# A linear-attention kernel with a GELU layer on one core: longer clock warm-up, tiled filler products, the first level's copy moved off VectorE, and a new order for the first two loops

## The chip, the core and the metric

The kernel runs on one core of a Trainium2 chip. The core has a matrix engine (TensorE, here PE; its weight loads are listed as PEld), a vector engine (VectorE, DVE), an engine for activations and copies (ScalarE, ACT), GpSimd (POOL) and SyncE (SP), which issues most of the transfers. Each engine works through its own instructions in the order in which the program emits them, and waits at semaphores for the others. The metric is the device time of one execution in microseconds (us), lower is better.

## What is computed

The first half is an attention without softmax: for each batch and head a 48 x 48 state decays by a factor per row and step, and takes in one outer product per step. The second half is a layer of two matrix products with an exact GELU between them.

```python
for t in range(S):                       # batch 4, heads 8, S = 768, D = 48
    kt, vt, rt, wt = (k[:, :, t], v[:, :, t], r[:, :, t], w[:, :, t])
    cur = np.einsum('bhd,bhe->bhde', u[None] * kt, vt)
    y[:, :, t] = np.einsum('bhd,bhde->bhe', rt, state + cur)
    state = wt[:, :, :, None] * state + np.einsum('bhd,bhe->bhde', kt, vt)
x = y.transpose(0, 2, 1, 3).reshape(3072, 384)
h = x @ w_in                             # 384 x 2048
out = (0.5 * h * (1.0 + erf(h / sqrt(2)))) @ w_out   # 2048 x 384
```

## The kernel before

**Tiles.** The 768 steps of each of the 4 batches are cut in two, so there are 8 tiles of 384 steps for all 8 heads (`x` from 0 to 7). `attention(x, unit)` computes the attention of one tile, `mlp(x)` the two products with the GELU behind it. Tile 0 is cut again into two units of four heads each (`units_of`), so that its parts can overlap while there is no other work yet; from tile 1 on a tile is one unit, and its attention runs beside the `mlp` of the tile before it.

**Attention.** Inside a chunk of 64 steps the matrix of scores is built by levels (`halves`, L469, for tiles 0 and 1): level h (1, 2, 4, 8, 16, 32) covers the pairs of steps in the two halves of blocks of 2h. For each level PE multiplies k by r in quadrants of 64 x 64 (`products`, L445), the needed part of the result `d` is copied from PSUM into the score matrix `a_sb`, and DVE multiplies r and k by the decay of their block (`update`, L493 to L505), so that the next level can use them in place. A level's update has to wait for its product, and the next product for the update. For levels 1 to 8 the copy is a predicated copy by DVE with a byte mask (L516); for levels 16 and 32 it is a row of plain copies by ACT (L513). The diagonal, with u, has a product of its own (L461) and a predicated copy (L465), which follows level 1's copy. Before the levels ACT scales r by u (L401) and DVE forms the products of the decays (L411). After them k is transposed (L685, copied by ACT at L687), multiplied with v (L711), the scores are multiplied with v (L752), DVE chains the states over the chunks (L726), and the states are multiplied with r (L797). The results go to `xT`: unit 0's by copies of ACT and DVE (L804), unit 1's by DVE copies (L820) and, for the heads whose rows are spread, through `ysb` (an ACT copy, L823) and six transfers (L827), three issued by SP and three by ACT.

**Fillers.** `keep_warm` (L219) issues products of a tile of zeros, 128 x 128 by 128 x 512, whose result nobody reads. Eight stand in front (L227), two behind each product of a level in tile 0 but the first (L457, twelve times in all), and six at the end of tile 0's loop.

**Weights.** They arrive as 64-bit floats in 16 pieces of 768 columns (8 of w_in, then 8 of w_out), with room for five (`raws`). A piece is brought in by `weight_in`, prepared by three ACT operations (`prepare`, L333 to L336) and finished by two DVE operations (`finish`, a shift at L345 and an add at L349). `conversion` runs these steps and, at its end, issues the piece that comes three later (L318). The first three pieces, and tile 1's r, k and w (`load_second`), are gated: a DVE memset of one column stands before each transfer, so that the transfer starts when DVE has come to that place. In tile 1's loop the products of w_in with a new piece need its add, and ACT's preparations stand in line with the GELUs of the same loop; two PSUM banks take turns under the products of h, so the product of one block waits until the GELU two blocks earlier has read its bank.

**Order.** `PLAN` (L39) holds a string per tile, written out by hand. Each letter runs one step of one stream, up to its next `yield`: for tile 0 "." is unit 0, "s" unit 1, "f" the attention of tile 1, "l" the gated loads, "c" the conversion of weights, "p" the preparation of pieces 1 and 2, "w" the load of tile 1's v, "x" the six fillers at the end. For later tiles "." is the `mlp` of the tile before, "s" the attention of this tile, "f" that of the next, "l" loads, "w" masks and sums, "x" sums of xT. The string fixes the order on every engine and on every queue.

Of the kernel before, what the change touches and what calls it, by code (L numbers as in the profile page):

```python
# [10 lines left out]
F32 = mybir.dt.float32  # L11
# [7 lines left out]
ALU = mybir.AluOpType  # L19
# [13 lines left out]
BANK = 512  # L33
# [3 lines left out]
NC_SP = 8  # L37
HALFWAY = 2
PLAN = {  # L39
    0: "l.s....llsl.lssslslss.lc.l.slslls...ssss..lcs.s.s.l.ss..ss..sccs.c.s.llpssslw..cs.ffpcc",  # L40
    1: (
        "..ccswccc.csl.scscs.s.sccwsc.clccs.ccsccc.csc.lscclswwclc.scs.wcssw.ss.cclcsc.ccs.lclccsc."
        "ccclfccccccfccfcccccfccfccwf.ff......fw.sl.w.x.wx...x..x...xww"
    ),
    2: (
        "s.s.....ss....ssw.ws.wl.wsss.wws.s..lsl...lws.w..s.ww....s.s..l..sss.lssss....s..s..s.sls."
        "llsf.sf.fs..fl.xx.x.fxx"
    ),
    3: (
# [24 lines left out]
def kernel(  # L74
# [9 lines left out]
    nc = tc.nc  # L84
# [16 lines left out]
    ps = ctx.enter_context(tc.tile_pool(name="ps", bufs=1, space=PSUM))  # L101
# [22 lines left out]
    half = [slice(0, 64), slice(64, 128)]  # L124
# [8 lines left out]
    bufs = [io.tile([128, 3 * NP * T], F32, name=f"rkw{i}", bufs=1) for i in range(2)]  # L133
# [58 lines left out]
    def weight_in(i, gate=False):  # L192

        if i < len(pieces):
            dst, src = pieces[i]
            raws[i] = cv.tile([128, PIECE], I64, name="raw", bufs=AHEAD) if wide else None
            if wide:
                dst = raws[i].rearrange("p (a c) -> p a c", a=dst.shape[1])
            if not gate:
                nc.sync.dma_start(out=dst, in_=src)  # L200
                return
            for a in range(dst.shape[1]):
                if wide:
                    nc.vector.memset(dst[:, a].bitcast(U32)[:, 0:1], 0)
                nc.sync.dma_start(out=dst[:, a], in_=src[:, a])
                yield
# [5 lines left out]
    zeros = const.tile([128, BANK], BF16, name="zeros")  # L212
    nc.vector.memset(zeros, 0.0)
    two = const.tile([128, 1], F32, name="two")
# [4 lines left out]
    def keep_warm(n, elsewhere=False):  # L219
        if elsewhere:  # L220
            t = pair("warm")[:, 0]
        else:
            t = ps.tile([128, BANK], F32, name="warm", tag="mm", bufs=2)
        for _ in range(n):
            nc.tensor.matmul(t, lhsT=zeros[:, 0:128], rhs=zeros, start=True, stop=True)

    keep_warm(8)  # L227


    masks = {h: const.tile([128, C // 2], U8, name=f"mask{h}") for h in LEVELS if h < 16}  # L230
# [37 lines left out]
    for i, h in enumerate(QUARTERS[:1]):  # L268
        for a in range(3):
            w_q = (3 - a) * C // 4  # L270
            z = q_ints[1 if a == 0 else 2]
# [35 lines left out]
    def conversion():  # L307

        i = converted[0]
        if i >= len(pieces):  # L310
            return
        converted[0] += 1

        prepare(i + HALFWAY if i > 1 else 0)
        yield
        if wide:
            yield from finish(pieces[i][0], raws[i], *halfway[i])
        for _ in weight_in(i + 3):  # L318
            pass

    def convert():
        for _ in conversion():
# [30 lines left out]
    def attention(x, unit):  # L353
# [7 lines left out]
        base = unit * 3 * n_u  # L361
# [3 lines left out]
        at = a_sb[:, :, parts[0] * NI:(parts[0] + np_) * NI]  # L365
# [79 lines left out]
        def products(bs, right, width, rest=False):  # L445
            d = pair("d")
            n = 0
            for b in bs:
                for i in range(NI):
                    for g in range(2):  # L450
                        for p in range(2):
                            nc.tensor.matmul(d[half[p], g, n * width:(n + 1) * width],  # L452
                                             lhsT=kc[half[g], b, i, p], rhs=right(half[g], b, i, p),
                                             start=True, stop=True)
                    n += 1
            if x == 0 and not rest:
                keep_warm(2)  # L457
            return d[:, :, 0:n * width]

        def diagonal():  # L460
# [8 lines left out]
        def halves():  # L469

            for h in LEVELS:
                m = C // 2 // h
                if np_ < NPART:

                    d = products(range(np_), lambda z, b, i, p: rc[z, b, i, p], C, h == 1)
                    d = d.rearrange("p g (n m two j) -> p g n m two j", two=2, j=h, m=m)[:, :, :, :, 1, :]
                else:
                    right = rc.rearrange("p b i c (m two j) -> p b i c m two j", two=2, j=h)[:, :, :, :, :, 1, :]
                    d = products(range(np_), lambda z, b, i, p: right[z, b, i, p], C // 2)
                    d = d.rearrange("p g (n m j) -> p g n m j", j=h, m=m)  # L480
                if h == 1:
                    yield
                    diag = diagonal()
                yield

                r2 = r.rearrange("p (n two j) -> p n two j", two=2, j=h)[:, :, 1, :]
                t2 = tot[h].rearrange("p (n two) -> p n two", two=2)[:, :, 0:1].to_broadcast(r2.shape)
                k2 = k.rearrange("p (n two j) -> p n two j", two=2, j=h)[:, :, 0, :]
                tk = tot[h].rearrange("p (n two) -> p n two", two=2)[:, :, 1:2].to_broadcast(k2.shape)
                rk = bass.AP(tensor=r2.tensor, offset=r2.offset, ap=[r2.ap[0], [n_u - h, 2]] + list(r2.ap[1:]))  # L490
                tt = bass.AP(tensor=t2.tensor, offset=t2.offset, ap=[t2.ap[0], [1, 2]] + list(t2.ap[1:]))

                def update(z, r2=r2, t2=t2, k2=k2, tk=tk):  # L493
                    nc.vector.tensor_mul(*((k2, k2, tk) if z is k else (r2, r2, t2)))

                if x == 0 and m == 1:

                    update(k)
                    last_r.append(lambda: update(r))
                elif x == 0 and h == 1:  # L500
                    update(r)
                    yield
                    update(k)
                else:
                    nc.vector.tensor_mul(rk, rk, tt)  # L505
                yield
                ah = at.rearrange("p g n (m two j) -> p g n m two j", two=2, j=h)[:, :, :, :, 1, :]
                if h >= 16:

                    for p in range(2):  # L510
                        for i in range(m):
                            s = slice(p * 64 + i * 2 * h, p * 64 + i * 2 * h + h)
                            nc.scalar.copy(out=ah[s, :, :, i], in_=d[s, :, :, i])  # L513
                else:
                    mask = masks[h].rearrange("p (m j) -> p m j", j=h).unsqueeze(1).unsqueeze(1)
                    nc.vector.copy_predicated(out=ah, mask=mask.to_broadcast(ah.shape), data=d)  # L516
                if h == 1:
                    copy_diagonal(diag)
                yield
# [186 lines left out]
        for b in range(np_):  # L706
            kv_ps = pair("kv_ps")
            for i in range(NI):
                for p in range(2):
                    for g in range(2):  # L710
                        nc.tensor.matmul(kv_ps[half[g], p, i * D:(i + 1) * D], lhsT=k_t(b, i, p, g),  # L711
                                         rhs=vs(b, i, g)[half[p], 0:D], start=True, stop=True)
# [74 lines left out]
        for i in range(NI):  # L787
            for p in range(2):
                for b in range(np_):
                    q, c3 = divmod(i, N3)  # L790
                    for g in range(2):
                        c = 2 * c3 + (p + g) % 2
                        src, c0 = (st, c - 1) if c else (before, NC - 1)
                        if src is None:
# [4 lines left out]
                                         start=False, stop=True, skip_group_check=True)  # L799
# [518 lines left out]
```

## Time and profile before

| | us |
|---|---|
| median of 3 runs | 588.55 (588.53 to 589.37) |
| the profiled execution | 589.61 |
| its span in the profile | 587.8 |
| PE busy, share of the span | 571.1 (97%) |
| DVE busy | 425.5 (72%) |
| ACT busy | 291.2 (50%) |
| POOL busy | 58.6 (10%) |
| PE's mean granted clock | 0.997 |

The span is the time between the first and the last instruction that the profile shows; 1.8 us of the execution lie outside of it. A row of the profile names a line of the kernel, the engine, the operation, and what it writes and reads. A 32-bit product leaves two records of PE, so the 24 products of one level of a unit are listed as x48. Starts are counted from the beginning of the span.

### The profile page before, as it was taken

Reading aid. Unit: us, or ns where it says so; the run is one execution under the profiler, and the core shown is the slowest. Engines: PE = TensorE matmul, PEld = TensorE weight load, DVE = VectorE, ACT = ScalarE, POOL = GpSimd, SP = SyncE. Lnnn points to the kernel's source line nnn. Section 1 sums busy time; section 2 is a strip of 40 time slices with the busy share of each in tenths; the row PEclk is TensorE's granted clock in tenths of the full one; section 3 lists DMA queues with packets and bytes.
Section 4 is the critical chain, followed back from the end, with each engine's and each line's share of the span. In section 5 each row is a group of like instructions: output and inputs, shape, how many; then the busy total and the mean of one; then the engine's idle time right before and its main releaser. Section 6 shows DMA issues by size and latency. Waiting matters only on the chain. (4 is left out here: it accounts for less than half of the span.)

```text
span 587.8 us, 17656 instructions
## 1 busy us (share of the span) xinstructions
PE 571.1 (97%) x7602; PEld 521.4 (89%) x7616; DVE 425.5 (72%) x825; ACT 291.2 (50%) x668; POOL 58.6 (10%) x63
## 2 busy tenths in 40 slices
PE   5789999999999999999999999999999999999997
PEld 3576666799999999999999999999998999999997
DVE  5988968989758975777959986777759987420332
ACT  2368898446362567235462467245561467335400
POOL 3100000013000130012000130002100111003100
PEclk8999999999999999999999999999999999999999
DMA  6749742253032542354122632344224333114201
GB/s 230 221 135 352 265 168 78 79 142 52 5 89 64 157 58 41 90 142 93 26 55 79 151 70 44 86 139 74 27 41 119 86 42 42 29 45 55 28 13 35
DMA packets 62430, 55.09 MB, mean 94 GB/s; under 512 B 32400, under 2 KB 47504, under 8 KB 62352
## 3 DMA queue, kind: packets, MB, share of 16 engines
q1 hardware_dynamic: 50832, 45.62, 25.5%
q0 software_dynamic: 11424, 8.26, 10.8%
q8 instruction: 60, 0.98, 0.7%
q14 instruction: 18, 0.15, 0.1%
q10 hardware_dynamic: 96, 0.07, 0.1%
HBM read 36.24 MB, written 4.72 MB: 70 GB/s over the span
## 5 line engine op out<-in xcount | busy, mean ns | idle before, releaser
L929 PE MATMUL h_ps<-xT,w_in_sb 128*128 128x192 f32 x560 | 111.5, 330 | 0.6 <-DVE o_sb L1196 0.6
L980 POOL DMA_DIRECT2D g<-o_sb x42 | 50.6, 1229 | 478.2 <-ACT o_sb L965 468.9
L929 PEld LDWEIGHTS h_ps<-xT,w_in_sb 128*128 128x128 f32 x560 | 93.0, 190 | 4.7 <-ACT g L961 1.6
L929 PE MATMUL u_ps<-s,w_in_sb 128*128 128x192 f32 x224 | 41.2, 327 | 0.0
L1073 PE MATMUL o_ps<-w_out_sb,g 128*128 128x192 f32 x224 | 39.8, 326 | 0.0
L929 PEld LDWEIGHTS u_ps<-s,w_in_sb 128*128 128x128 f32 x224 | 37.1, 190 | 0.2
L1073 PEld LDWEIGHTS o_ps<-w_out_sb,g 128*128 128x128 f32 x224 | 37.0, 190 | 0.0
L604 ACT COPY a_sb<-d 32x256 f32<-32x256 f32 (+8 forms) x90 | 32.6, 362 | 4.9 <-PE d L588 3.4
L1059 PE MATMUL h_ps<-xT,w_in_sb 128*128 128x384 f32 x96 | 33.2, 494 | 0.0
L452 PEld LDWEIGHTS d<-rkw 64*64 64x64 f32 x1152 | 19.4, 138 | 14.7 <-issue 10.5
L1073 PE MATMUL o_ps<-w_out_sb,f 128*128 128x192 f32 x176 | 32.0, 331 | 0.0
L1073 PE MATMUL o_ps<-t,g 128*128 128x192 f32 x176 | 31.4, 330 | 0.0
L1073 PE MATMUL o_ps<-t,s 128*128 128x192 f32 x176 | 31.2, 328 | 0.0
L1073 PE MATMUL o_ps<-t,e 128*128 128x192 f32 x176 | 30.6, 326 | 0.5 <-issue 0.5
L621 DVE COPY_PREDICATED a_sb<-quarter,d 128x480 f32<-128x480 uint8 (+5 forms) x54 | 23.2, 439 | 10.5 <-PE d L588 9.3
L726 DVE SCALAR_TENSOR_TENSOR st<-st,tot_sb,kv_ps 128x48 f32<-128x48 f32 x160 | 28.9, 258 | 2.6 <-PE kv_ps L711 2.5
L1073 PE MATMUL o_ps<-w_out_sb,e 128*128 128x192 f32 x176 | 30.7, 328 | 0.0
L982 DVE TENSOR_TENSOR g<-g,o_sb 128x384 f32<-128x384 f32 x14 | 7.6, 549 | 31.2 <-ACT o_sb L965 31.1
L1073 PEld LDWEIGHTS o_ps<-t,e 128*128 128x128 f32 x176 | 28.9, 190 | 0.7 <-issue 0.7
L1073 PEld LDWEIGHTS o_ps<-t,g 128*128 128x128 f32 x176 | 28.6, 190 | 0.5
L1073 PEld LDWEIGHTS o_ps<-w_out_sb,f 128*128 128x128 f32 x176 | 28.5, 190 | 0.6
L1073 PEld LDWEIGHTS o_ps<-t,s 128*128 128x128 f32 x176 | 28.8, 190 | 0.2
(163 smaller groups left out, 1171.3 us busy)
## 6 DMA issues: line engine op xcount, KB each, us to landing
rkw<-in_rkw_dram SPq DMA_DIRECT2D x54, 256.0 KB, 3.6
g<-o_sb POOLq DMA_DIRECT2D x42, 192.0 KB, 3.6
raw<-in_w_out_dram SPq DMA_DIRECT2D x8, 768.0 KB, 6.2
v_in<-in_v_dram SPq DMA_DIRECT2D x8, 584.0 KB, 4.6
raw<-in_w_in_dram SPq DMA_DIRECT2D x5, 768.0 KB, 7.5
out_dram<-o_sb SPq DMA_DIRECT2D x20, 192.0 KB, 2.0
rkw<-kx SPq DMA_DIRECT2D x72, 48.0 KB, 2.0
rkw<-in_rkw_dram SPq DMA_DIRECT2D x6, 384.0 KB, 6.2
```

The source lines that it names most:

```text
L452: nc.tensor.matmul(d[half[p], g, n * width:(n + 1) * width], lhsT=kc[half[g], b, i, p], rhs=right(half[g], b, i, p), start=True, stop=True)
L604: nc.scalar.copy(out=at[z, g, first:behind, (a + 1) * h:], in_=d[z, :, :, to] if g == slice(None) else d[z, :, to])
L621: nc.vector.copy_predicated(out=an[:, :, :, :, (a + 1) * h:], mask=mask.to_broadcast(data.shape), data=data)
L726: nc.vector.scalar_tensor_tensor(out=stq[:, q, c], in0=stq[:, q, c - 1] if c else b4[:, q, NC - 1], scalar=totq[:, q, c:c + 1], in1=kvs[q ...
L929: nc.tensor.matmul(o, lhsT=lhsT, rhs=rhs, start=start, stop=True, skip_group_check=True)
L980: nc.gpsimd.dma_start(out=g, in_=z, accum_op=ALU.add)
L982: nc.vector.tensor_add(g, g, z)
L1059: nc.tensor.matmul(h_ps, lhsT=w_in_sb[:, f // FI, j, f % FI * 128:(f % FI + 1) * 128], rhs=xT[:, j, :], start=(j == 0), stop=(j == NJ - 1))
L1073: nc.tensor.matmul(o, lhsT=lhs(j), rhs=rhs(j), start=start and j == 0, stop=(j == HF - 1), skip_group_check=True)
```

## The change

- `keep_warm(24)` in front instead of `keep_warm(8)`.
- The twelve fillers between the levels of tile 0 are four products of 64 x 64 by 64 x 512 each, one in each quadrant of PE, on two banks (`keep_warm_tiles`), instead of two products over the whole array.
- Level 1 in tile 0: the predicated copy by DVE goes. ACT copies the odd columns of `d` into `a_sb` without a mask, and two affine selects of POOL (64 partitions and 384 columns each, one for each half) set to zero what lies below the diagonal; what they leave above it is overwritten by later levels. The diagonal's copy by DVE follows them.
- The fourth piece of weights (number 3) is issued at the end of the second conversion, together with the fifth, instead of at the end of the first.
- The strings of `PLAN` for tiles 0 and 1 are new; that of tile 2 differs in its first slots.

```diff
@@ PLAN @@
-    0: "l.s....llsl.lssslslss.lc.l.slslls...ssss..lcs.s.s.l.ss..ss..sccs.c.s.llpssslw..cs.ffpcc",
+    0: ".s..l.l.lsll..ssl.lslclslls.cs.s.sl.ls.sc.ssspsl..s.sslsl...s.sc.css.l.ccpws.sss..s.cff",
     1: (
-        "..ccswccc.csl.scscs.s.sccwsc.clccs.ccsccc.csc.lscclswwclc.scs.wcssw.ss.cclcsc.ccs.lclccsc."
-        "ccclfccccccfccfcccccfccfccwf.ff......fw.sl.w.x.wx...x..x...xww"
+        ".wcsccc..c.scwssccc.ccsccsl.cwscscs.lll.ccccccss.scccscc.csc.sscsc.clscl.s.ccsc.cscswc.ccl"
+        "llcccflsccw.c.fc.cwccxxc...fwf.x.cc.cf.cc.f......f..fwxfw.wxww"
     ),
     2: (
-        "s.s.....ss....ssw.ws.wl.wsss.wws.s..lsl...lws.w..s.ww....s.s..l..sss.lssss....s..s..s.sls."
+        ".s......sss...ssw.ws.wl.wsss.wws.s..lsl...lws.w..s.ww....s.s..l..sss.lssss....s..s..s.sls."
...
+    def keep_warm_tiles():
+        ts = [ps.tile([128, BANK], F32, name="warm", tag="mm", bufs=2) for _ in range(2)]
+        for p in range(2):
+            for g in range(2):
+                nc.tensor.matmul(ts[g][half[p]], lhsT=zeros[half[g], 0:64], rhs=zeros[half[g]], start=True, stop=True)
-    keep_warm(8)
+    keep_warm(24)
...
-        for _ in weight_in(i + 3):
-            pass
+        for n in (() if i == 0 else (3, 4) if i == 1 else (i + 3,)):
+            for _ in weight_in(n):
+                pass
...
             if x == 0 and not rest:
-                keep_warm(2)
+                keep_warm_tiles()
...
+                ah = at.rearrange("p g n (m two j) -> p g n m two j", two=2, j=h)[:, :, :, :, 1, :]
+                if h == 1 and x == 0:
+                    nc.scalar.copy(out=ah, in_=d)
+                    for z in half:
+                        a1 = ah[z, :, :, :, 0]
+                        nc.gpsimd.affine_select(out=a1, in_=a1, pattern=[[0, 2], [0, a1.shape[2]], [2, m]], base=1,
+                                                channel_multiplier=-1, compare_op=ALU.is_ge, fill=0.0)
...
-                ah = at.rearrange("p g n (m two j) -> p g n m two j", two=2, j=h)[:, :, :, :, 1, :]
                 if h >= 16:
...
-                else:
+                elif h > 1 or x:
                     mask = masks[h].rearrange("p (m j) -> p m j", j=h).unsqueeze(1).unsqueeze(1)
                     nc.vector.copy_predicated(out=ah, mask=mask.to_broadcast(ah.shape), data=d)
```

Read letter by letter, the new strings move the following. In tile 0, the first gated load of weights moves from the very front behind both units' decay products and unit 0's first two products. Unit 0's diagonal copy stands before unit 1's first update, and unit 0's product of level 2 before unit 1's diagonal product. The preparation of piece 1 stands on ACT before the copies of level 16, and that of piece 2 before `ysb`, where they stood behind the copy of the transposed k and behind tile 1's first steps. In tile 1's loop, the add of piece 1 follows the first block of h, pieces 3 and 4 are issued behind it, and the preparation of piece 3 stands before the GELU of the second block. The products of states with r (L797) come before the first product of the second layer, where they came behind nine of them. The sums of weights and of xT are spread later in the loop.

## The prediction

> **What bounds the kernel now.** I read the busy shares first, then the waits of TensorE (PE), then the timeline of the first 60 us.
>
> ```profile
> PE 571.1 (97%) x7602; PEld 521.4 (89%) x7616; DVE 425.5 (72%) x825; ACT 291.2 (50%) x668; POOL 58.6 (10%) x63
> ...
> PE   5789999999999999999999999999999999999997
> ```
>
> PE is busy everywhere except in the first three slices (14.7 us each). Its waits between 40 and 120 us are one of 0.5 us, and after 112 us 1.8 us in all; from 41.5 us (the first products of tile 1) it is a solid block. So the change can gain only what it brings this block forward, and lose what holes it makes in it. TensorE's waits of the first 50 us:
>
> ```profile
> PE d L452 <- DMA rkw<-in_rkw_dram: 3.5, 1, 3.5
> PE warm L225 <- ACT zeros L217: 2.3, 1, 2.3
> PE d L452 <- issue: 1.8, 2, 1.4
> PE kv_ps L711 <- issue: 1.0, 1, 1.0
> ```
>
> "issue" is a wait that no semaphore explains. TensorE's timeline shows where:
>
> ```profile
> 2.29 3.59 PE L225 MATMUL warm<-zeros 128*128 128x512 bf16 x8 [2.29 <-ACT zeros L217]
> 9.43 1.56 PE L452 MATMUL d<-rkw 64*64 64x64 f32 x48 [3.55 <-DMA rkw<-in_rkw_dram]
> ...
> 18.76 0.91 PE L452 MATMUL d<-rkw 64*64 64x64 f32 x45 [0.22 <-DVE rkw L163]
> 21.09 0.33 PE L452 MATMUL d<-rkw 64*64 64x64 f32 x3 [1.42 <-issue]
> ...
> 28.09 0.93 PE L452 MATMUL d<-rkw 64*64 64x64 f32 x48
> 28.95 0.39 PE L225 MATMUL warm<-zeros 128*128 128x512 bf16 x1
> 29.48 0.93 PE L452 MATMUL d<-rkw 64*64 64x64 f32 x48
> ```
>
> The first product takes 1.56, later ones 0.93. The breaks come at 699, 953 and 1717 PE instructions (matmuls plus weight loads, counted from the timeline): 254 and three times 254.7 apart. The instruction queue moved 60 packets, 0.98 MB, so 16 KB each; over the 15,218 matmuls and loads that is 64 bytes an instruction and 256 a packet. In windows of 0.2 us those packets start at 12.8, 18.6, 22.2, 26.6, 30.0, 35.0, mostly 1.0 us after a boundary; PE resumes 4.8 us after one (16.3 to 21.09), 4.5 (21.09 to 25.55), and a boundary at 29.0 passes 3.45 us after. So in this stage PE uses at most a block per 3.4 to 4.8 us, the longer ones while the data queue is full.
>
> Between 14 and 30 us VectorE (DVE) is the other bound: busy 4.97, 4.53 and 4.42 of each 5 us from 15 to 30.
>
> **The clock in front.** Windows of 1 us (seventh figure: granted clock):
>
> ```profile
> 9.00:10.00 1.00, 0.57 (x21) 0.60 (x25) 0.00 (x0) 0.56 (x2) 0.00 (x0) 0.68 0.99 402
> 10.00:11.00 1.00, 1.00 (x50) 1.00 (x46) 0.00 (x0) 0.74 (x2) 0.00 (x0) 0.50 0.85 339
> 12.00:13.00 1.00, 0.67 (x13) 0.22 (x6) 0.67 (x5) 0.00 (x0) 0.00 (x0) 0.61 0.18 62
> 13.00:14.00 1.00, 0.93 (x49) 0.82 (x49) 0.97 (x2) 0.00 (x0) 0.00 (x0) 1.00 0.05 16
> ```
>
> Half clock from 9.36 to 12.78 us, 3.42 us long, after 3.55 us of idleness. Loads of the eight fillers are 0.427 us apart; warm ones 0.216 (six from 43.09 end where the next product starts, 44.40). If the clock rises at 5.95, one span before 9.36, 24 products end at 2.29 + 3.66 + 15.4 x 0.216 = 9.3, just before the data (9.43). The first two products then cost 0.93 each, not 1.56 and 1.54: unit 0's second ends at 11.3, not 12.3. [...] A start up to 10.4 stays hidden behind ScalarE (ACT), below.
>
> **Level 1 by ACT and POOL.** Removed from DVE: two predicated copies of 1.02. Added: two ACT copies of 384 columns (0.48, the row of ysb), four affine selects of 64 x 384.
>
> ```profile
> masks.py:199 POOL TENSOR_SCALAR_AFFINE_SELECT ident<-ident 128x128 f32<-128x128 f32 x1 | 0.3, 295 | 0.1
> L289 POOL COPY rkw<-ident 32x128 f32<-32x128 f32 x4 | 2.4, 589 | 0.2
> ```
>
> The 16-element iota takes 0.17, so 128 elements cost 0.13 of the 0.295 above it; 384 give 0.17 + 0.39 = 0.56. From the strided copy (0.589 per 128) 1.6; from the plain memset (1.38 per 1536) 0.4. I take 0.58, the same operation; two in a row 1.16, bounds 0.8 to 3.2. Unit 0's ACT copy stands behind unit 1's scaling by u, which waits for its r and ends at 11.38 (10.26 + 1.12): 11.38 + 0.48 + 1.16 + 0.2 for two hand-overs = **13.2**. DVE has finished unit 0's updates at 11.9, and its diagonal copy waits there; behind it in order are unit 1's r update and, through that, everything. So 1.3 us of the 2.1 saved return as a wait; with 3.2 all of it and more. Unit 1's selects end at about 14.4, its diagonal copy is due at 16: hidden.
>
> From 13.2, by start-to-start times of the rows (diagonal 0.94, r and k 0.48 each, level 2 updates 0.9, copies 0.9): eight operations, 6.45, end at 19.65 against 21.40 before. Then, for DVE alone, the level 4 and 8 updates and copies (2.8 a level) and the first shift (0.5) end at 25.75, and the last two levels alternate with PE: 29.3 for unit 0's last k update (31.88 before).
>
> **Fillers in tiles.** Twelve times two full products become four 64 x 64 ones. Lower bound 0.22 (side by side), upper 0.86 (in a row). The 48 records of d take 0.93, though 64 columns at the h rate (0.345 per 384) in a row would take 2.76: quadrants do run beside each other. I take 0.25. A step of PE shrinks from 1.395 (28.09 to 29.48) to 1.17, but only where PE sets the pace (26 to 32 us: five steps, 1.1). At upper cost five steps lose 2.
>
> **Instruction blocks.** The change adds 32 instructions in front and 4 per filler, 80 by the end of the levels. Counted back from 699, boundaries lie at 187, 443 and so on. With 48 instructions of fillers and 96 of the first product ahead, 187 is passed at 10.8, inside unit 0's second product (43 of 96), and its block is there at 14.8; 443, reached at 13.5 (after unit 1's first product and unit 0's level 2), waits for it; then 19.1, 23.1, 26.6, 30.1, taking 4.0, 4.3, 4.0, 3.5 and 3.5 from the cycles above, as the loads now fill 11 to 20 us. The boundary at 30.1 lies in the last product of the levels, so its k update starts at 30.3, before 31.88: **1.6 earlier**. DVE alone would reach it at 29.3. [...]
>
> **Loads moved, weights, ACT's queue.** The first weight gate goes behind both totals (DVE 3.2 to 7.7 us; SP 4.57 to about 7.7). The loads land in issue order (k of unit 0 at 9.4, r of unit 1 at 10.2, v 12.6, weights 13.5), so I count 0, at most 0.4. All 17 gates remain, 0.06 each. The second conversion is prepared before the level 16 copies (weights there by 22, ACT done by 25, copies due at 26: hidden). The third preparation (2.95 on ACT) now stands before ysb. Its last third is gated behind the first add: 30.8 + 0.95 = 31.75, landing 3.0 to 3.8 later (35.3), prepared at 38.2. The cross products end at 37.1; so ysb starts at 38.2, before 39.57; behind it on ACT are three xT loads (2.18) and unit 0's xT copies. xT lands 1.4 earlier; PE's own path (chains, cross products, tile 1, six fillers) gives h at 42.4 to 42.8 against 44.40. I take 42.8: **1.6**.
>
> **Tile 1's loop.** Weight piece 3, issued at 30.48 before, now follows the xT loads on SP, at 40.2, and pieces 4 to 7 with it. Its preparation stands on ACT before the gelu of h1, which frees the bank of h3. First of a string, a piece lands after 6.1 or 6.6: 46.6; prepared 49.5, gelu 49.9; h3 is due at 42.8 + 3 x 2.05 + 1.55 = 50.5. Hidden by 0.6. Later, shift 4 waits on DVE for the piece prepared behind h3's gelu; eleven DVE operations follow (11.6) before the level 16 products, due 14.9 after h3; 0.43 + 2.88 + 12.05 = 15.4. I count 0.05 of the possible 0.5, since overlaps of 0.1 per operation undo it. Weights of the second layer: last add about 0.7 us ahead of need, counted 0. Tile 2's order changes only in its first slots: 0.
>
> Sum: -1.6 + 0.05 = -1.55. The profiled execution took 589.61 (span 587.8, 1.8 around it), the median of runs 588.55; a change in the span applies to both. 588.55 - 1.55 = **587.0**.
>
> **Rivals and chances.** Forecast, 0.50: -0.8 to -2.4 (586.15 to 587.75).
> Fetch hides, 0.20: the k update at 29.3, add done 30.75, weights 34.3, ysb 37.2; h at 42.1, 586.2, down to 585.0 if POOL also is quick (1.3 less wait). For it: no break at 29.0 and 34.2. Against: three breaks.
> The gain is spent, 0.17: POOL at 3.2 us (ready at 15.2) delays DVE by 2.0, partly behind PE's block wait; or the hole of 0.5 and small ones. 587.8 to 589.7.
> Slower, 0.13: piece 3 lands late, sharing the queue with pieces 4 to 7 and v. Rows of later pieces are 8.5 and 9.9 us. Decisive from 6.9 after issue (47.1); each us beyond is a us of hole before h3; break-even at 8.5, at 9.9 it costs 3.0 and gives 590.0.
> That the fillers do not warm the clock is part of these: 24 products span 5.2 us even warm.
>
> A measurement here can tell 0.2%, 1.2 us. Faster: 0.7 of the forecast plus the second, 0.55; slower 0.13 and a little of the third, 0.14; same 0.31. The range leaves out the far end of the second (0.05) and most of the fourth: 585.4 to 588.9.
>
> **What would show it.** Right: first product near 9.4 and 0.93 long; a DVE wait of about 1.3 on POOL before the first diagonal copy; breaks of PE 256 instructions apart; ysb right behind the third preparation; h from about 42.8, no PE wait after. Wrong: selects over 1 us each, fillers past 10.4, or a PE wait on the gelu before h3.

## The result: slower by 0.85%

| | before | after |
|---|---|---|
| median of five runs each, us | 588.85 (588.53 to 589.37) | 594.51 (592.88 to 594.53) |
| the profiled execution | 589.61 | 592.88 |
| its span | 587.8 | 591.2 |

The ratio is 1.0085 [1.0072, 1.0098]. The forecast was 587.0 and the range ended at 588.9: wrong, and on the other side. The profiled executions lie only 3.3 us apart, because the traced run of before is longer than any of its five and that of after is its shortest. What follows explains the 3.4 us between the two spans; the further 2 us of the medians rest on runs without a trace, and come up again under the clock.

The busy shares of the changed kernel, as shown for before:

```profile
PE 572.6 (97%) x7654; PEld 522.3 (88%) x7656; DVE 423.8 (72%) x823; ACT 292.1 (49%) x670; POOL 61.0 (10%) x67
...
PE   7679999999999999999999999999999999999997
```

DVE has lost 1.7 us of work, as meant. PE is fuller in the first slice (7 tenths instead of 5) and emptier in the next two (6 and 7 instead of 7 and 8); over the whole span its share is 97% in both. What is lost shows in TensorE's waits (what, released by what: total, times, longest):

```profile
PE d L460 <- issue: 6.5, 5, 1.8
PE warm L225 <- ACT zeros L217: 2.4, 1, 2.4
PE y_ps L813 <- issue: 1.3, 1, 1.3
PE d L460 <- DVE rkw L522: 0.8, 1, 0.8
PE kv_ps L727 <- issue: 0.8, 1, 0.8
PE warm L232 <- issue: 0.7, 1, 0.7
PE h_ps L1075 <- issue: 0.6, 1, 0.6
```

The wait of 3.5 us for the first data is gone, since the 24 products now fill it. In its place stand waits for "issue", which no semaphore explains: nine breaks and 9.8 us in the first 80 us, where before had five and 3.2 (two of these, 0.5 us together, stand ahead of fillers and belong to no boundary). TensorE's timeline shows where they lie (start, busy, what it is, how many, and the idle time ahead of it):

```profile
2.37 8.06 PE L225 MATMUL warm<-zeros 128*128 128x512 bf16 x24 [2.37 <-ACT zeros L217]
10.35 0.93 PE L460 MATMUL d<-rkw 64*64 64x64 f32 x48
...
14.95 0.40 PE L232 MATMUL warm<-zeros 64*64 64x512 bf16 x2 [0.67 <-issue]
...
20.05 0.62 PE L460 MATMUL d<-rkw 64*64 64x64 f32 x25 [1.78 <-issue]
...
24.05 0.27 PE L460 MATMUL d<-rkw 64*64 64x64 f32 x1 [1.35 <-issue]
...
31.39 0.28 PE L460 MATMUL d<-rkw 64*64 64x64 f32 x4 [0.94 <-issue]
...
36.13 0.80 PE L727 MATMUL kv_ps<-v_in,kx 64*64 64x48 f32 x41 [0.76 <-issue]
...
40.13 1.33 PE L813 MATMUL y_ps<-rkw,st 64*64 64x64 f32 x39 [1.33 <-issue]
...
43.87 0.36 PE L460 MATMUL d<-rkw 64*64 64x32 f32 x9 [1.10 <-issue]
...
52.15 3.71 PE L1075 MATMUL h_ps<-xT,w_in_sb 128*128 128x384 f32 x11 [0.57 <-issue]
...
72.96 0.89 PE L460 MATMUL d<-rkw 64*64 64x32 f32 x44 [1.31 <-issue]
```

Each break falls inside a row of equal products, never between two steps, so missing data does not explain it: the next record of the same row is held back. Counted over products and weight loads in the trace, the breaks stand at 445, 701, 957, 1467, 1719, 1975, 2231, 2478 and 3240. So they follow each other at 256 instructions, or at about a multiple of it where a boundary passes without a break (at about 28, 61.5 and 67.5 us); a few records are missing from a trace. The instruction queue again moved 60 packets of 16 KB, and each of the nine breaks ends 2.3 to 2.7 us after one of these packets has started (at 17.66, 21.44 and 28.96 for the breaks that end at 20.05, 24.05 and 31.39).

How far each stage is behind or ahead (starts in us):

| | before | after | difference |
|---|---|---|---|
| first product | 9.43 | 10.35 | +0.9 |
| unit 0's diagonal copy | 13.89 | 13.47 | -0.4 |
| first level 4 update | 21.46 | 20.76 | -0.7 |
| unit 0's last k update | 31.88 | 31.80 | -0.1 |
| `ysb` | 39.57 | 40.38 | +0.8 |
| first block of h | 44.40 | 45.47 | +1.1 |
| fifth block of h | 55.52 | 57.31 | +1.8 |
| tile 2's first product (u) | 118.36 | 122.10 | +3.7 |
| the last row of the second layer | 554.92 | 558.28 | +3.4 |

The saving of the levels is eaten by four breaks inside them (15 to 32 us). Then three breaks between the levels and h, 3.2 us long, cost a net 1.1, since before had a break of 0.96 and a wait of 0.52 in the same stretch. The loop of tile 1 costs another 2.7: from the first h to tile 2's u it takes 76.63 instead of 73.96. Its two breaks are 1.88 of idle time and cost 2.0 with the restart; this is the difference to after_full_apart (below), which has full fillers, the same string but for one step, and no break there. That run still takes 74.62, so 0.66 belongs to the new string itself, half of it in one row of products of the scores with v (1.97 long instead of 1.63). After 122 us nothing is lost any more.

### The profile page after: what moved, and what is told of

The parts are those of the page before. It is cut to its first block, busy times and chain, and to the rows that moved or that the text cites. A ratio compares the mean times of both kernels' runs of the same rounds, so it can differ in the third digit from the quotient of the medians.

```text
span 591.2 us, 17753 instructions
## 1 busy us (share of the span) xinstructions
PE 572.6 (97%) x7654; PEld 522.3 (88%) x7656; DVE 423.8 (72%) x823; ACT 292.1 (49%) x670; POOL 61.0 (10%) x67
## 5 line engine op out<-in xcount | busy, mean ns | idle before, releaser
L460 PE MATMUL d<-rkw 64*64 64x64 f32 (+1 forms) x1152 | 22.3, 221 | 8.1 <-issue 6.5
```

Of the source, the lines that this page charges most:

```text
L460: nc.tensor.matmul(d[half[p], g, n * width:(n + 1) * width], lhsT=kc[half[g], b, i, p], rhs=right(half[g], b, i, p), start=True, stop=True)
```

## Experiments

**Theory A:** PE gets its instructions at no more than a block of 256 per 3.5 to 4 us; the change shifts the boundaries, and adds instructions, so that they fall into dense rows on the path. **Rivals:** B, the tiled fillers themselves take too long; C, they fail to hold the clock; D, the new order of tile 0 or tile 1 loses, whatever the fillers; E, the blocks come late because the data transfers crowd them out. Medians below are of several runs, and each ratio is against before on the same chip. Single runs of one kernel differ by 1.5 to 7.4 us, so only intervals decide. The "issue" column and the starts are of one traced run each.

### Which part of the change costs

The changed kernel once more, and parts of it undone:

> The changed kernel itself, beside the others on one chip: 593 to 594.5 (ratio 1.006 to 1.009); PE breaks of the kind issue of 8 to 11 us in all.

> After, with the old strings of tiles 1 and 2. Theory (blocks of 256 PE instructions that arrive no faster than one per 3.4 to 5.5 us, which the change asks for faster): the hole of 1.31 at 73 us comes from two level products (384 records and loads) only 2.0 us apart, the one of 0.57 at 52 from the late fourth piece; with the old string the level products are 5.6 us apart again, the first hole goes, and the second may stay because the piece is still issued behind xT: 1.3 to 1.9 less than after. Rival (everything is lost before 45 us): same as after within 0.3.

> After, with the old string of tile 0 (its loads and steps in the old order), all else new. Theory of blocks: the fillers and their 80 instructions stay, so PE still breaks every 256 instructions; the data loads of 11 to 20 us come later again, so the breaks get shorter: 0 to 1.5 less than after. Rival (the new order of tile 0 is what costs): h starts about 1 earlier than in after and 1.5 to 3 of the loss goes.

> After, with the twelve fillers between the levels as two full products again. Theory of blocks: 48 instructions fewer before the end of the levels, breaks of PE shorter by about 0.7 in all and others moved: 0.5 to 1.5 less than after. Rival (tiled fillers do not keep the clock up, which is what the runs with a mean clock of 0.988 to 0.997 and spans of 592.8 show): clock 0.997 or more in all runs and 1.5 to 3 less. Second rival (tiled fillers help): 0.5 to 1.5 more, since PE steps of 1.17 become 1.4.

> After, with 8 products in front. In after the 24 end at 10.43 and hold back data that is there by about 9. Theory (the front is a loss of its own): first product 0.9 to 1.4 earlier, but at half clock (1.56 and 1.54 instead of 0.93), 32 instructions fewer: net 0 to 1.5 less than after. Rival (warm clock is worth it): 0.5 to 1.5 more than after.

> After, with the full fillers and the old strings of tiles 1 and 2: what is left of the change is 24 products in front, level 1 by ScalarE and GpSimd, the late fourth piece and the new string of tile 0. Theory of blocks: both places where blocks ran short are gone; -1 to +0.5 against before, breaks under 4 us in all. Rival (new order of tile 0 costs by itself): +1.5 to +3 against before.

```diff
 after_old_loop1:       PLAN[1] and PLAN[2] of before
 after_old_loop0:       PLAN[0] of before
 after_full_fillers:
-                keep_warm_tiles()
+                keep_warm(2)
 after_8_in_front:
-    keep_warm(24)
+    keep_warm(8)
 after_full_old_loop1:  full fillers, and PLAN[1], PLAN[2] of before
```

| | median | ratio [95%] | "issue" to 80 us | first h | tile 2's u |
|---|---|---|---|---|---|
| after_again | 594.14 | 1.0081 [1.0051, 1.0111] | 9.2 | 46.75 | 124.85 |
| after_old_loop1 | 590.72 | 1.0033 [1.0011, 1.0054] | 7.6 | 45.00 | 119.60 |
| after_old_loop0 | 596.28 | 1.0114 [1.0076, 1.0153] | 11.5 | 47.49 | 127.42 |
| after_full_fillers | 590.20 | 1.0022 [0.9997, 1.0046] | 3.9 | 45.20 | 124.78 |
| after_8_in_front | 590.77 | 1.0022 [1.0003, 1.0041] | 5.6 | 44.74 | 120.40 |
| after_full_old_loop1 | 588.93 | 0.9997 [0.9970, 1.0025] | 3.0 | 43.70 | 117.76 |

(The traced run of after_full_fillers was by far its longest, 594.99; its stations count little.)

The loss repeats. Three different edits each take back about 3 us of it (2.8 to 3.5 by the ratios, more than I had expected of any of them): other fillers, the old loop of tile 1, or 16 products (32 instructions) fewer in front. Two of them together take back about 5, all of it, less than the sum of the two. That speaks against a cost that sits in one part, and for one resource that all of them draw on or shift. The new string of tile 0, suspected by rival D, is not shown to lose: with the old one the kernel is no faster (1.0114, four runs, an interval that overlaps that of after_again), where I had expected up to 1.5 us less. Everything else in the change (24 in front, level 1 by ACT and POOL, the later fourth piece, tile 0's order) is together worth nothing that can be measured, 0.9997.

### Instructions, or time of the fillers

> After, with one 64 x 64 product per filler instead of four (2 instructions instead of 8; the same 0.2 us, as the four run side by side). Theory of blocks: 72 instructions fewer before the end of the levels, each stretch between breaks holds more work, 1.5 to 3 less than after. Rival (time of fillers or clock matters): the array is used a quarter as much, so the clock falls more often (mean 0.99 or less) and the time is the same as after or 1 to 3 more.

> Before, with two narrow products of zeros (two columns, 128 x 128) added behind each of the twelve fillers: 8 instructions per filler, as many as the tiled ones, and about 0.1 us of PE. Theory of blocks: breaks grow by about 48 instructions' share of a block (0.7 us) and move: 0.5 to 2 more than before. Rival (instructions do not matter): no more than the 0.1 per step where PE sets the pace, 0 to 0.5 more.

> After, with fillers of two full products and two narrow ones (two columns): 8 instructions like the four tiles, but 0.5 us on the array instead of 0.2. If the tiles lose by their instructions: as after (593 to 594.5), breaks of 8 us or more. If they lose by their short time (a block of 256 instructions is used up before the next is there, PE idles, the clock falls): near after_full_fillers (590 to 591.5), breaks under 5, clock mostly 1.0.

> After with full fillers, and 24 narrow products (64 x 64, two columns, 48 instructions, some 0.5 us in a stretch in which PE waits for ScalarE's copy of the transposed k) in front of unit 1's kv. The levels run as in after_full_fillers, but behind them the boundaries lie where after has them. If the place decides: breaks again with 41, 39 and 9 records left in kv, in the products of the states and in tile 1's first product, and with 44 in tile 1's level 16, 3 to 5 us in all; 1.5 to 3.5 more than after_full_fillers, 591.7 to 593.7. If their number in the levels decides: within 0.7 of after_full_fillers.

```diff
 after_one_tile (one 64 x 64 product per filler, 2 instructions instead of 8):
-        for p in range(2):
-            for g in range(2):
+        for p in range(1):
+            for g in range(1):
 before_more_instructions (before), after_full_padded (after, two full products): 8 instructions per filler
+            nc.tensor.matmul(t[:, 0:2], lhsT=zeros[:, 0:128], rhs=zeros[:, 0:2], ...)   # twice
 after_full_shifted (full fillers; after the transposes of unit 0's k in tile 0, 48 instructions):
+                for _ in range(24):
+                    nc.tensor.matmul(t[half[0], 0:2], lhsT=zeros[half[0], 0:64], rhs=zeros[half[0], 0:2], ...)
```

| | median | ratio [95%] | "issue" to 80 us | first h | tile 2's u |
|---|---|---|---|---|---|
| after_one_tile | 591.79 | 1.0029 [0.9995, 1.0062] | 4.5 | 43.26 | 118.81 |
| before_more_instructions | 590.18 | 1.0005 [0.9979, 1.0032] | 2.4 | 44.62 | 118.58 |
| after_full_padded | 595.18 | 1.0097 [1.0059, 1.0134] | 6.4 | 45.58 | 123.54 |
| after_full_shifted | 594.29 | 1.0084 [1.0053, 1.0115] | 6.1 | 45.42 | 122.73 |

after_one_tile, with fewer instructions, takes back 2.4 us by the medians, as expected; the intervals still touch. after_full_padded has the full fillers, which alone were at 1.0022, and the instruction count of the tiled ones. It is as slow as the changed kernel, though its breaks come to 6.4 us, less than the 8 that I had expected, and it breaks at the same records behind the levels (41, 39, 9 and 44 left, compare the timeline above):

```profile
36.80 0.80 PE L733 MATMUL kv_ps<-v_in,kx 64*64 64x48 f32 x41 [0.77 <-issue]
...
40.25 1.33 PE L819 MATMUL y_ps<-rkw,st 64*64 64x64 f32 x39 [0.79 <-issue]
...
43.99 0.36 PE L465 MATMUL d<-rkw 64*64 64x32 f32 x9 [1.10 <-issue]
...
72.72 0.89 PE L465 MATMUL d<-rkw 64*64 64x32 f32 x44 [1.43 <-issue]
```

after_full_shifted leaves the fillers of the levels alone and puts the 48 missing instructions at a place where PE waits for ACT's copy of k anyway. That wait is only 0.23 us, so they hold kv back by about 0.4. The breaks come back, one record further on, and with them the whole loss (the expectation had 591.7 to 593.7):

```profile
36.59 0.84 PE L731 MATMUL kv_ps<-v_in,kx 64*64 64x48 f32 x42 [0.94 <-issue]
...
40.31 1.33 PE L817 MATMUL y_ps<-rkw,st 64*64 64x64 f32 x40 [1.06 <-issue]
...
43.77 0.41 PE L460 MATMUL d<-rkw 64*64 64x32 f32 x10 [0.72 <-issue]
...
73.59 0.89 PE L460 MATMUL d<-rkw 64*64 64x32 f32 x45 [1.46 <-issue]
```

So rival B falls: the time of the tiled fillers costs nothing that these runs show, their instructions do. And it is not their number as such: before takes the same number per filler without a measurable loss (I had expected 0.5 to 2 more; the interval runs from -1.2 to +1.9). There, 32 instructions fewer stand ahead (8 products in front), and the boundaries lie elsewhere. What decides is which row a boundary falls into.

The sum of the breaks does not decide: after_full_shifted, with 6.1, is as slow as the changed kernel with 9.8, and after_old_loop1, with 7.6, is faster than both. Among the runs built from the changed kernel, the breaks behind the levels come nearer. They are 4.1 to 5.1 us in after, after_again, after_old_loop0, after_full_padded and after_full_shifted (ratios 1.0081 to 1.0114), 2.0 to 2.9 in after_old_loop1, after_one_tile and one_full_old_loop1 (1.0029 to 1.0043), and 1.0 or less in after_full_fillers, after_full_apart, after_full_old_loop1 and full_old_loop1_18 (0.9997 to 1.0022). after_light_loads, with 4.5 at 1.0048, and after_8_in_front, with 3.9 at 1.0022, lose less than that order gives them. It is an order seen afterwards, in one trace each, and no test.

### Late blocks, or busy transfers

> After, with tile 1's r, k and w loaded only in 64 of 576 columns of each share (2.4 MB less through the data queue between 13 and 27 us; the rest of the tile is zeros written in front by ScalarE, so tile 1's attention is not that of the reference). Same instructions on PE. Theory of blocks whose fetch stands in the data queue: the breaks between 14 and 25 us (1.8 and 1.35 in after, 1.64 and 2.45 in its second profile) fall to under 0.8 each, the transposed k and with it kv comes 1.5 to 3 earlier than 33.65. Rival (a fixed time per block, whatever the data do): breaks as in after, kv within 0.7.

```diff
-            dma.dma_start(out=bufs[1][:, s], in_=rkw[1, :, s])
+            few = slice(s.start, s.start + 64)
+            dma.dma_start(out=bufs[1][:, few], in_=rkw[1, :, few])
...
+    nc.scalar.copy(out=bufs[1], in_=zeros[:, 1:2].to_broadcast([128, 3 * ALL]))
```

Measured 591.92, 1.0048 [1.0023, 1.0074], "issue" 9.2, h 45.28, u 121.61. From 12 to 35 us the transfers now fill 0.34 of the queues instead of 0.62, and from 25 to 30 us 0.04. The breaks stay, though not each one (the first grows to 2.19, and that at 20 us is gone):

```profile
23.87 0.27 PE L463 MATMUL d<-rkw 64*64 64x64 f32 x1 [1.40 <-issue]
...
31.49 0.28 PE L463 MATMUL d<-rkw 64*64 64x64 f32 x4 [0.94 <-issue]
...
36.49 0.80 PE L730 MATMUL kv_ps<-v_in,kx 64*64 64x48 f32 x41 [1.03 <-issue]
...
43.69 0.36 PE L463 MATMUL d<-rkw 64*64 64x32 f32 x9 [1.07 <-issue]
```

PE goes on after breaks at 23.87, 27.87, 31.49 and later at 36.49, 39.95, 43.69: 4.0 and 3.6, then 3.5 and 3.7 apart. Rival E, which I held myself before this run, falls for this stage: a block took 3.5 to 4.0 us in this run, and 4.0 of them (23.87 to 27.87) beside an almost idle data queue. The run came out 2 us faster than the changed kernel, but the intervals overlap, so whether its data transfers cost something in another way is not shown.

### The hole in tile 1's loop

> After with full fillers, and in tile 1's string one step moved: the product of level 16 goes behind the ninth block of h instead of in front of it, so that two blocks of h lie between the products of levels 8 and 16. Theory (two level products 2 us apart use up a block early): the hole of 1.0 to 1.4 at 71 to 76 us is gone, and -0.7 to -1.5 against after_full_fillers (590.2). Rival (the hole is a late weight or GELU): hole stays at 0.8 or more.

```diff
 PLAN[1], with full fillers: the product of level 16 behind six more records of h
-        ".wcsccc..c.scwssccc.ccsccsl.cwscscs.lll.ccccccss.scccscc.csc.sscsc..."
+        ".wcsccc..c.scwssccc.ccsccsl.cwscscs.lll.ccccccss.sccccc.scsc.sscsc..."
```

Measured 590.08, 1.0005 [0.9983, 1.0026], "issue" 3.0, and no "issue" wait after 36 us. Its tile 1 levels:

```profile
64.55 1.60 PE L442 MATMUL d<-rkw 64*64 64x32 f32 x96
66.08 4.14 PE L1057 MATMUL h_ps<-xT,w_in_sb 128*128 128x384 f32 x12
70.14 1.60 PE L442 MATMUL d<-rkw 64*64 64x32 f32 x96
71.68 2.20 PE L1057 MATMUL h_ps<-xT,w_in_sb 128*128 128x384 f32 x6
73.81 1.60 PE L442 MATMUL d<-rkw 64*64 64x32 f32 x96
```

In the changed kernel level 16 follows level 8 after 2.2 us of h, and the second boundary, in level 16, is reached about 4.2 us after the first, in level 8 (67.5 to 71.65). The block comes at 72.96, 5.5 after the first: its packet starts at 70.6, while the transfers of weights take 0.79 of all queues from 60 to 70 us. Here 4.1 us of h lie between, and the boundary passes unnoticed, though levels 16 and 32 are now as close together as 8 and 16 were: no boundary pair falls badly there. From the first h to tile 2's u it takes 74.6 instead of 76.6 (before: 74.0). Since the fillers differ too, and the break in h at 52 us is gone as well, the 2.0 are not the work of the moved step alone; the break in level 16 is 1.31. In the whole time the step is not resolved: 1.0005 against 1.0022 for after_full_fillers, with intervals that overlap. The 0.66 us over before that are left without a break are what holds of rival D for tile 1.

### The clock, and a candidate for a better version

> The rest of the change (24 in front, level 1 by ScalarE and GpSimd, late piece, new string of tile 0) with the old strings of tiles 1 and 2 and with one full product per filler: as long on the array as the four tiles side by side, 4 instructions instead of 8. Theory A (tiles lose the clock because their breaks leave PE idle): breaks 2 to 4 in all, mean clock 0.997 to 1.0, -0.5 to -2 against before. Theory B (0.2 us per filler is too little for the clock gate, tiled or not): clock 0.99 to 0.997 in most runs, +0.5 to +2 against before.

> As after_full_old_loop1 (full fillers, old strings of tiles 1 and 2) with 18 products in front: they end at 8.2 to 9.1 instead of 9.2 to 10.4, before or at the arrival of the data (about 9.0). Theory (24 hold the first product back by up to 1.4): -0.3 to -1.2 against after_full_old_loop1 and before. Rival (level 1's wait hides the start up to 10.4): 0 within 0.3.

> Before, with one full product per filler. Theory of blocks: 24 instructions fewer, a PE step of 1.17 where it sets the pace; 256 instructions then last 3.0 us, so about half of the 1.1 us of pace comes back as breaks: 0 to -1 against before. Rival (clock): +0.5 to +2, with more runs at 0.994 or less.

> Before, with one full product per filler, again beside the others: 587.5 to 588.5 and -0.3 to -1.5 against before if the shorter PE steps hold; if the first comparison was chance, within 0.3 of before.

> Before, with 18 products in front, all else old. Theory (the front saves the half clock of the first two products, 1.2 us, of which the later waits hide a part): -0.3 to -1.2 against before. Rival (20 more instructions move the boundaries and take it back): within 0.3 of before, or up to 1 more.

> Before, with one full product per filler and 18 products in front. Theory: the first two products run at full clock (1.2 less), 20 instructions more (0.2): -0.5 to -1.5 against before_one_full, 586.8 to 588. Rival (the front is hidden behind the r and k of unit 1, and the blocks take the gain): within 0.4 of before_one_full.

```diff
 one_full_old_loop1 (from after_full_old_loop1), before_one_full, before_one_full_again:
-                keep_warm(2)
+                keep_warm(1)
 full_old_loop1_18: keep_warm(18) in front instead of 24; before_18: 18 instead of 8
 before_one_full_18: both, keep_warm(18) in front and keep_warm(1) between the levels
```

| | median | ratio [95%] | "issue" to 80 us | first h | tile 2's u |
|---|---|---|---|---|---|
| one_full_old_loop1 | 591.89 | 1.0043 [1.0024, 1.0063] | 5.6 | 46.87 | 121.54 |
| full_old_loop1_18 | 588.34 | 0.9997 [0.9971, 1.0022] | 3.8 | 44.10 | 118.20 |
| before_one_full | 588.09 | 0.9989 [0.9970, 1.0008] | 3.2 | 42.56 | 117.24 |
| before_one_full_again | 588.00 | 0.9980 [0.9958, 1.0002] | 4.6 | 47.37 | 122.26 |
| before_18 | 588.20 | 0.9978 [0.9953, 1.0004] | 3.3 | 43.58 | 117.54 |
| before_one_full_18 | 588.95 | 0.9969 [0.9945, 0.9994] | 3.3 | 41.61 | 115.57 |

(The traced run of before_one_full_again was its longest, 593.32, with a break of 3.00 that ends at 39.47 and half the clock from 8.36 to 15.19 and from 39.08 to 42.50 us; every later stage starts 5 us later than in before_one_full.) One full filler instead of two is harmless in before's order, and costs 0.46% in the changed one (1.0043 against 0.9997), where it also saves 24 instructions. That is what the clock's theory in its expectation had: nine of its twelve runs have a mean clock of 0.994 or less. In its trace two breaks, 1.85 at 20.35 and 2.54 at 38.18, are each followed by a stretch at half the clock. The same shows in the trace of after_again behind its longest break:

```profile
24.96 0.37 PE L460 MATMUL d<-rkw 64*64 64x64 f32 x1 [2.45 <-issue]
```

and in its windows (busy time of PE, PEld, DVE, ACT, POOL, then the granted clock):

```profile
22.00:24.00 2.00, 0.51 (x34) 0.37 (x26) 1.82 (x5) 0.42 (x1) 0.00 (x0) 1.00 0.81 226
24.00:26.00 2.00, 1.04 (x28) 1.04 (x32) 0.53 (x1) 1.97 (x3) 0.00 (x0) 0.68 0.36 135
26.00:28.00 2.00, 1.57 (x42) 1.00 (x34) 1.25 (x2) 0.46 (x1) 0.00 (x0) 0.50 0.00 0
```

A stretch of 3.4 us at half the clock lowers the mean of a run by 0.003. Of the changed kernel's 15 runs, in two rounds of measurement, one kept 1.000 and eleven had 0.994 or less; in after_full_fillers nine of ten kept 1.000. So rival C is real as a companion: the clock falls behind many of the long breaks. Full fillers do not rule that out: of the eight runs of after_full_padded and after_full_shifted, which have them too, one kept 1.000. The clock is not needed for the loss: the traced run of the changed kernel kept 1.000 and is 3.4 us longer than that of before, and after_full_shifted had three runs at 0.997 and one at 1.000, and was as slow.

It does bear on the further 2 us of the medians. The trace of after_again is 2.2 us longer than that of after, though its breaks come to 0.6 less. Its clock was at half from 24.70 to 31.53 and from 75.90 to 79.31 us. In the second stretch twelve records of h take 5.76 to the start of the next row, instead of 4.07:

```profile
74.84 5.83 PE L1075 MATMUL h_ps<-xT,w_in_sb 128*128 128x384 f32 x12
```

In the ten runs of after_again the time goes with the mean clock: 590.94 and 591.61 at 0.997, 592.88 to 594.28 at 0.994, 593.92 to 596.22 at 0.991 and 0.989. The first five runs of the changed kernel do not follow it (1.000, 0.991, 0.988, 0.997, 0.994, at 592.88, 593.63, 594.51, 594.53, 594.51). So how the loss of a run divides between breaks and clock stays open.

before_one_full_18 is the one variant whose whole interval lies below before: 0.9969, and well below the changed kernel. It takes from the change only the idea that the wait for data in front can be filled, and one product less per filler. The former alone (before_18) gives 0.9978 and the latter alone 0.9989 and 0.9980, each with an interval that includes 1. That it beats before is likely and not settled: the interval ends at 0.9994 and is the best of eighteen, and its median, 588.95, stands beside 589.66 for before and 588.00 for before_one_full_again on the same chip. In the changed kernel's order 18 products in front instead of 24 gained nothing (0.9997 with both), where I had expected 0.3 to 1.2 us.

## Why the prediction was wrong, point by point

- **Instruction blocks: the failing step.** The mechanism was the right one, and the paragraph that priced it stopped too early. It forecast PE's blocks at 14.8, 19.1, 23.1, 26.6 and 30.1. PE went on at 14.95, 20.05, 24.05, about 28 and 31.39: cycles of 5.1, 4.0 and 7.3 for the last two, where I took 4.3, 4.0 and 7.0. So the last k update came at 31.80, not 30.3. That alone would have made the change worth nothing. Then I followed the boundaries no further than the levels. The next ones fall into kv (0.76), ahead of the last of the 40 records that unit 1's products with the states have (1.33), into tile 1's first product (1.10), into h (0.57) and into level 16 (1.31). None of the five was in the sum, which counted the way from the levels to h and tile 1's loop without a break. after_full_shifted and after_full_padded show that these places are what costs.
- **`ysb` behind the third preparation: wrong releaser.** That preparation ended at 39.3 (forecast 38.2), but ACT waited on for PE, whose last products were held back by the break at 40.13:

```profile
38.25 1.06 ACT L344 ACTIVATE e<-raw 128x768 f16<-128x768 f32 x1
40.38 0.48 ACT L839 COPY ysb<-y_ps 128x384 f32<-128x384 f32 x1 [1.06 <-PE y_ps L813]
```

- **h at 42.8: missed by 2.7.** 1.5 of it come from the levels, the rest from the breaks at 36, 40 and 44 us.
- **Tile 1's loop, counted at 0.05: wrong.** It cost 2.7, of which 2.0 go with the two breaks and 0.66 with the string itself (74.62 in after_full_apart, without a break, against 73.96). I checked the data of each step (pieces, GELUs, shifts) and not the distance of dense products. Piece 3, the mechanism of the slower rival, was later than forecast (landed about 48.9 against 46.6, the GELU behind it, of h1, done at 52.3), but h was later too, and h3 came at about 53.9 (52.15 plus five records of 0.345) with no wait. The break at 52.15 lies one record into h2, whose bank the GELU of h0 had left at 48.2. The rival gave the right sign for a reason that did not come true.
- **The clock in front: partly right.** The first product takes 0.93 instead of 1.56, as forecast. But the clock rose late in this execution, at 7.87 and not at 5.95: the 24 products took 8.06 and ended at 10.4, just the bound that I had called hidden. In after_full_apart they took 6.65 and the first product started at 9.24.
- **Level 1 by ACT and POOL: right in the time it is ready, wrong in the wait.** Four selects took 2.76, or 0.69 each (0.58 taken), ready at about 13.4 (13.2). DVE's wait was 0.45, not 1.3, since its own updates were late, one of them by the late start and by 0.94 beside POOL:

```profile
12.05 0.94 DVE L511 TENSOR_TENSOR rkw<-rkw 128x384 f32<-128x384 f32 x1
...
13.47 1.02 DVE L473 COPY_PREDICATED a_sb<-mask,d 128x768 f32<-128x768 uint8 x1 [0.45 <-POOL a_sb L507]
```

- **Fillers in tiles: right in time, wrong in kind.** They passed quickly beside other products: at 11.80 and at 17.48 the next product starts 0.22 after them (0.25 taken). Their price was the four instructions more that each brings.
- **The second rival, fetch hides, was the wrong doubt.** I gave 0.20 to fetch costing nothing and no chance to its costing more than in the levels. The rival missing from the list was this one: the shifted boundaries fall into dense rows behind the levels. The places were to be had from the trace of before: counted on at 256 from 699, with 80 instructions more, each boundary has a row, and dense rows with less than 4 us since the last boundary were the ones to price. How long each break would be was not: the same boundaries cost 0.57 and 0.25 in h in two traces of the changed kernel.

## What to carry to other kernels

Where an engine's trace shows breaks that no semaphore explains, count its instructions: if the breaks are 256 apart, a block of instructions is a resource with a price (3.5 to 4.0 us each in after_light_loads, and 5.5 once in the changed kernel, beside transfers that filled 0.79 of the queues), and each edit that adds instructions moves every later boundary. Count such an edit through to where the engine has slack again, not only to the end of the stage that is edited. A filler of two long products was cheaper in that resource than one of four short ones (4 instructions against 8; breaks of 3.9 us in after_full_fillers, 9.8 in the changed kernel), and a break behind which the clock fell cost twice (1.40 us at 74.02 in after_again, then 5.76 instead of 4.07 for a row of h).

## What the runs showed of the hardware

- A block of 256 PE instructions took 4.0 us from one resumption to the next where the transfers filled only 0.04 of the queues (23.87 to 27.87 in after_light_loads), and 3.5 to 3.7 in three later stretches of that run (to 31.49, 39.95 and 43.69).
- The breaks ended at a nearly fixed distance from a packet: all eleven of 0.5 us or more in the first 80 us of before and after ended 2.3 to 2.7 us after the start of a 16 KB packet on the instruction queue, and the five of after_light_loads between 15 and 40 us ended 2.1 to 2.9 after one, read from windows of 0.2 us.
- The clock fell to half for 3.4 us (6.8 in after_again, from 24.70) behind some breaks, from 1.40 (after_again, 74.02) to 3.00 us (before_one_full_again, 39.47), but not behind 1.78 (after, 20.05) or 1.91 (after_full_padded, 19.89).
- Two-input operations of DVE on 384 columns took 0.94 and 0.77 while POOL's affine selects ran, 0.57 and 0.56 otherwise (after).
- The same 24 products of zeros from the same start took 6.65 in after_full_apart and 8.06 in after, and between 6.65 and 8.12 in the twelve traces that have them. In after the clock rose at 7.87, with 0.427 us a product before and 0.216 behind it; from these the rise in after_full_apart lies at about 5.0, an estimate.
- ACT began scaling r at 7.53 in after and at 8.44 in before; I had counted 0, at most 0.4. That the moved load of weights did it is not shown by these two traces.
